# A Hedgehog attention and GLU kernel: the exponentials of the k features as 32 small ScalarE activations per tile, with bias and accumulator

## The chip, the core and the metric

The program runs on one core of a Trainium2 chip. The metric is the device time of one execution in microseconds (us); less is better. The core has five engines, each with its own instruction queue that is worked off in order: TensorE (PE, matmuls), VectorE (DVE), ScalarE (ACT), GpSimd (POOL) and SyncE (SP), which here issues nearly all DMA transfers. An instruction that waits holds up everything behind it on its engine.

## The reference

```python
xn = layernorm(x)                                   # x: 2048 x 1024
q, k, v = split_heads(xn @ wqkv)                    # 32 heads of 32 columns
pq, pk = q @ w_phi, k @ w_phi                       # per head, 32 x 32
phi_q = concat(softmax(pq), softmax(-pq))           # per head: 64 features
phi_k = concat(softmax(pk), softmax(-pk))
kv, z = phi_k^T v, sum_s phi_k                      # per head, over all 2048 rows
s = ((phi_q kv) / (phi_q z + 1e-6)) @ wo
g = silu((sigmoid(xn @ w_gate) * (xn @ w_up)) @ w_down)   # inner width 3584
out = x + s * g
```

The change concerns the two softmaxes of `pk` alone: for each row and head, exp(p - max p) and exp(min p - p) over 32 columns, and the sum of each.

## The kernel before

Everything is fp32. A matrix operand is split into a rounded high part (`L128`, a ScalarE copy) and the rest (`L129`, a VectorE subtraction), and each product takes three matmuls (`mm3`, lines 133 to 135). Each large product is done by seven half-size products (named B11, T2, B21, T3, T1, T4, B22) of sums of blocks; GpSimd makes the sums.

The work runs in stages, with PE's matmuls as the frame: the projections v, k, q of the first half of the rows (chunk 0, from about 20 us), the gate and up products of chunk 0 (28 units of seven ops), the same two stages for chunk 1 (the second gate stage ends at about 1675 us), the down projection with the gate's silu, and attention with the output projection. In the first two kinds of stages PE uses four PSUM banks, in the down projection all eight.

One op of a gate unit is 12 matmuls into one bank. In a unit, B11's sum is copied out of PSUM by ScalarE (`L855`), then B21 accumulates into the same bank, with T2 between them; likewise T4 follows T3 into its bank after VectorE has read it (`L859`), and B22 follows T1 (`L867` or `L874`). Weights stand up to eight ops ahead in a ring of slots.

Small work is spread between the ops as background tasks, by a table of due times (`background`, called behind an op of the gate stage): `k_task` (32 of them, 16 row tiles times 2 halves of 512 columns), `q_features` (32), sums of weights and turns of x. A `k_task` loads a tile of k (`kraw`, one buffer) and of v by DMA, has `features` make the exponentials into `e_k` (one buffer) and the reciprocals of their sums, multiplies, splits features and v into operands and adds the features to `zacc`. The eight matmuls of its products (`L475`) are traced when the next background task begins, and go to the other four PSUM banks. After the last task of a half come `kv_sum`, `kv_blocks` and `z_broadcast`, which use these four banks too.

`features` works on 16 heads of 32 columns, 128 rows: maximum and minimum per head (`L425`, `L426`, VectorE reductions to 128x16), two subtractions of 128x512 with the maximum or minimum broadcast (`L434`, `L435`), one ScalarE exponential of 128x1024 (`L436`), one sum to 128x32 (`L438`) and its reciprocal (`L439`). For k the result lies head by head, first sign and second sign side by side.

A scheduler orders each engine's queue, from the order in which the program is traced and its own estimate of times; so the queues are not in the order of the code. On ScalarE an exponential and a sigmoid need different tables, loaded by an ACT_TABLE_LOAD of 1.28 us.

## Time and profile before

| | before |
|---|---|
| median of 3 runs | 2423.59 us (2423.05 to 2424.21) |
| profiled execution, its own time | 2425.68 us |
| its span, first to last instruction | 2423.9 us |
| granted TensorE clock over the span | 0.993 |
| busy: PE, DVE, ACT, POOL | 97%, 73%, 41%, 41% |
| exponentials of k (`L436`, tile `fc`): 32 | first at 231.8 us, last at 1596.5 us |

A row of a group of instructions gives line, engine, operation, tiles (out <- in, buffer numbers left out), shapes and count, then busy us and the mean ns of one, then the engine's idle time before them and what ended it. A row of a single line gives durations as min/median/max in ns and the first and last start in us. A row of waits gives who waited for whom, the total in us, how often, and the longest. Tile names are those of the slots: `w` weights, `x` the operands of x, `fa`, `fb`, `fc` and `p` the small buffers, `bank` PSUM, `stk` and `stq` the small tiles of k and q features. Durations of neighbours on one engine overlap a little.

### The profile page before, as it was taken

What the parts mean: (1) busy time and instruction counts of PE and PEld (TensorE: products, weight loads), DVE (VectorE), ACT (ScalarE), POOL (GpSimd) and SP (SyncE); (2) the same over time, 40 slices, a digit from 0 to 9 for tenths busy, and PEclk for the clock granted to TensorE, in tenths of its full rate; (3) what the DMA queues carried; (4) which work ended last, traced back from release to release, by engine and by line L of the source; (5) the groups of instructions that cost most, each with busy time, mean ns of one, the idle gap of its engine ahead of it and who ended that gap; (6) DMA issues with size and microseconds to landing.
All of it is one profiled execution on the core that took longest, in us unless ns stands there. A gap on an engine that the chain in (4) does not pass through costs nothing. (4 is left out here: it accounts for less than half of the span.)

```text
span 2423.9 us, 31722 instructions
## 1 busy us (share of the span) xinstructions
PE 2359.0 (97%) x10728; PEld 1952.8 (81%) x10728; DVE 1760.6 (73%) x2341; ACT 996.8 (41%) x1484; POOL 1001.3 (41%) x638
## 2 busy tenths in 40 slices
PE   6999999999999999999999989999999999999998
PEld 4888878788888888887888777878888888788887
DVE  7535797778688764388858998865768786667885
ACT  6432345444454442234534443434333333255442
POOL 4530154757566442002343534343333334322655
PEclk9999999999999999999999999999999999999999
DMA  7874467888888798457898978789668766878664
GB/s 275 268 265 158 160 223 245 287 288 295 302 289 289 260 326 309 154 197 272 301 355 288 310 258 291 263 273 358 212 219 268 244 212 219 279 250 285 215 213 157
DMA packets 262323, 626.17 MB, mean 258 GB/s; under 512 B 37904, under 2 KB 58384, under 8 KB 257552
## 3 DMA queue, kind: packets, MB, share of 16 engines
q1 hardware_dynamic: 262160, 624.15, 75.0%
q8 instruction: 84, 1.38, 0.2%
q14 instruction: 79, 0.65, 0.1%
HBM read 374.47 MB, written 249.56 MB: 257 GB/s over the span
## 5 line engine op out<-in xcount | busy, mean ns | idle before, releaser
L133 PE MATMUL bank<-x,w 128*128 128x512 f32 x2352 | 911.1, 392 | 24.6 <-DVE fc L859 10.0
L134 PE MATMUL bank<-x,w 128*128 128x512 f32 x2352 | 919.4, 391 | 0.0
L135 PE MATMUL bank<-x,w 128*128 128x512 f32 x2352 | 910.1, 391 | 0.0
L129 DVE TENSOR_TENSOR w<-fa,w 128x512 fp32r<-128x512 f32 (+1 forms) x444 | 442.4, 1000 | 215.1 <-ACT w L128 197.1
L133 PEld LDWEIGHTS bank<-x,w 128*128 128x128 f32 x2352 | 443.9, 189 | 124.8 <-DVE fc L859 12.4
L128 ACT CAST w<-fa 128x512 fp32r<-128x512 f32 (+1 forms) x444 | 308.7, 698 | 527.4 <-PE bank L134 348.3
L135 PEld LDWEIGHTS bank<-x,w 128*128 128x128 f32 x2352 | 443.9, 189 | 92.6
L134 PEld LDWEIGHTS bank<-x,w 128*128 128x128 f32 x2352 | 444.3, 189 | 91.5 <-DVE x L129 0.4
L135 PE MATMUL bank<-w,x 128*128 128x512 f32 x708 | 278.1, 393 | 5.8 <-DVE x L129 5.8
L133 PE MATMUL bank<-w,x 128*128 128x512 f32 x708 | 278.5, 394 | 3.2 <-ACT x L128 1.8
L134 PE MATMUL bank<-w,x 128*128 128x512 f32 x708 | 277.4, 392 | 0.0
L613 POOL TENSOR_TENSOR fc<-fc 128x1024 f32<-128x1024 f32 x32 | 82.0, 2563 | 258.4 <-DMA fc<-e_d 116.2
L875 POOL TENSOR_TENSOR fb<-fb,fc 128x512 f32<-128x512 f32 x57 | 90.8, 1592 | 203.1 <-DVE fc L874 203.1
L135 PEld LDWEIGHTS bank<-w,x 128*128 128x128 f32 x708 | 133.7, 189 | 35.4 <-DVE x L129 7.8
L133 PEld LDWEIGHTS bank<-w,x 128*128 128x128 f32 x708 | 133.7, 189 | 32.0 <-ACT x L128 3.0
L134 PEld LDWEIGHTS bank<-w,x 128*128 128x128 f32 x708 | 133.9, 189 | 26.4
L129 DVE TENSOR_TENSOR x<-fa,x 128x512 fp32r<-128x512 f32 x112 | 113.8, 1017 | 36.0 <-ACT x L128 36.0
L334 POOL TENSOR_TENSOR fb<-fa 128x512 f32<-128x512 f32 x28 | 41.8, 1491 | 229.3 <-DMA fa<-w_gu 133.5
L875 POOL TENSOR_TENSOR fc<-fc 128x512 f32<-128x512 f32 x27 | 41.0, 1518 | 230.1 <-ACT w L128 172.4
L129 DVE TENSOR_TENSOR w<-fb,w 128x512 fp32r<-128x512 f32 (+1 forms) x114 | 112.9, 992 | 15.0 <-ACT w L128 14.8
L128 ACT CAST w<-fb 128x512 fp32r<-128x512 f32 (+1 forms) x114 | 70.9, 624 | 120.0 <-PE bank L134 80.9
L128 ACT CAST x<-fa 128x512 fp32r<-128x512 f32 x112 | 69.4, 620 | 75.7 <-DMA fa<-wd_d 38.9
(241 smaller groups left out, 3243.3 us busy)
## 6 DMA issues: line engine op xcount, KB each, us to landing
ws_d<-w SPq DMA_DIRECT2D x112, 512.0 KB, 4.4
w<-ws_d SPq DMA_DIRECT2D x112, 512.0 KB, 5.5
fa<-w_gu SPq DMA_DIRECT2D x84, 512.0 KB, 5.1
fa<-h_d SPq DMA_DIRECT2D x84, 512.0 KB, 4.7
fa<-wf_d SPq DMA_DIRECT2D x32, 1024.0 KB, 5.6
h_d<-fc SPq DMA_DIRECT2D x120, 256.0 KB, 4.6
h_d<-fb SPq DMA_DIRECT2D x76, 256.0 KB, 4.2
fc<-qkv_d SPq DMA_DIRECT2D x64, 256.0 KB, 4.3
```

The costliest lines, as they stand in the source:

```text
L128: nc.scalar.copy(o[0], src)
L129: return nc.vector.tensor_sub(o[1], src, o[0].bitcast(F32))
L133: nc.tensor.matmul(o, a[0], b[0], start=first, stop=False, **kw)
L134: nc.tensor.matmul(o, a[0], b[1], start=False, stop=False, **kw)
L135: nc.tensor.matmul(o, a[1], b[0], start=False, stop=last, **kw)
L334: nc.gpsimd.tensor_add(s1, a21, a22)
L613: nc.gpsimd.tensor_mul(ez, e, zb)
L875: nc.gpsimd.tensor_mul(g, g, b)
```

## The change

For k the two subtractions, the one exponential and the sum are replaced. The maximum is negated (128x16), and then for each of the 16 heads and both signs one ScalarE activation reads 32 columns of the raw k tile, multiplies by 1 or -1, adds the negated maximum or the minimum of its row as bias, takes the exponential and writes the row's sum by the accumulator output. That is 32 activations of 128x32 a task, 1024 in all. For q nothing changes but the place in the code. From line 427 on, line numbers after the change are larger, by 4 from `nc.vector.reciprocal` (`L443`) to the end.

```diff
+        s2, r2 = [st[:, a:a + 2].rearrange("p t h -> p (t h)") for a in (2, 0)]
         if query:
             ev = e.rearrange("p (a t h d) -> p t a h d", a=2, t=2, d=DH)
             pv, mx, mn = [a.rearrange("p (a h) d -> p a h d", a=2) for a in
                           (pv, mx[:, :, None].to_broadcast([P, nh, DH]), mn[:, :, None].to_broadcast([P, nh, DH]))]
+            nc.vector.tensor_tensor(ev[:, 0], pv, mx, op=ALU.subtract)
+            nc.vector.tensor_tensor(ev[:, 1], mn, pv, op=ALU.subtract)
+            nc.scalar.activation(e, e, AF.Exp)
+            nc.vector.tensor_reduce(s2, e.rearrange("p (g d) -> p g d", d=DH), axis=AX.X, op=ALU.add)
         else:
-            ev = e.rearrange("p (h t d) -> p t h d", t=2, d=DH)
-            mx, mn = [a[:, :, None].to_broadcast([P, nh, DH]) for a in (mx, mn)]
-        nc.vector.tensor_tensor(ev[:, 0], pv, mx, op=ALU.subtract)
-        nc.vector.tensor_tensor(ev[:, 1], mn, pv, op=ALU.subtract)
-        nc.scalar.activation(e, e, AF.Exp)
-        s2, r2 = [st[:, a:a + 2].rearrange("p t h -> p (t h)") for a in (2, 0)]
-        nc.vector.tensor_reduce(s2, e.rearrange("p (g d) -> p g d", d=DH), axis=AX.X, op=ALU.add)
+            nc.vector.tensor_scalar(mx, mx, -1.0, None, op0=ALU.mult)
+            ev = e.rearrange("p (g d) -> p g d", d=DH)
+            for h in range(nh):
+                for t, b, scale in ((0, mx, 1.0), (1, mn, -1.0)):
+                    g = 2 * h + t
+                    nc.scalar.activation(ev[:, g], pv[:, h], AF.Exp, bias=b[:, h:h + 1], scale=scale, accum_out=s2[:, g:g + 1])
         nc.vector.reciprocal(r2, s2)
```

The scheduler lays out the queues anew. Three places show it. On ScalarE, in the second gate stage, around the exponential of one k task (`fc` to `fc`; `fb` to `fb` is a q feature's, `p` takes the split of features and of v, `bank_98` holds B11 and then B21), before:

```order
L855 COPY fc_97<-bank_98 128x512
L128 CAST w_93<-fa_95 128x512
L436 ACTIVATE fc_97<-fc_97 128x1024
L128 CAST p_6009<-fc_97 128x8x64
L436 ACTIVATE fb_96<-fb_96 128x1024
L865 ACT_TABLE_LOAD
L865 ACTIVATE fc_97<-bank_98 128x512
```

and of the change, from one B11 copy (`L859` now) to the next:

```order
L859 COPY fc_97<-bank_98 128x512
L128 CAST w_93<-fa_95 128x512
L442 ACTIVATE fc_97,stk_9753<-fc_97,stk_9753 128x32 x32
L128 CAST p_6241<-fc_97 128x8x64
L869 ACT_TABLE_LOAD
L869 ACTIVATE fc_97<-bank_98 128x512
L872 ACTIVATE fb_96<-fb_96 128x512 x2
L128 CAST w_93<-fa_95 128x512 x2
L872 ACTIVATE fc_97<-fc_97 128x512
L434 ACT_TABLE_LOAD
L434 ACTIVATE fb_96<-fb_96 128x1024
L128 CAST p_6241<-fc_97 128x8x128
```

The 32 activations stand as one run behind the B11 copy, in nearly every unit of that stretch, and the unit's sigmoids and most of its casts stand behind them.

On PE, where the last k task's products (`L475`) stand, before, amid the gate stage (`x_0_90,w_93` are B11's operands there, `x_1_642` is one of the next op's):

```order
L135 MATMUL bank_98<-x_0_90,w_93 128x512
L475 MATMUL bank_102<-p_6009 128x256 x2
L475 MATMUL bank_103<-p_6009 128x256 x2
L475 MATMUL bank_104<-p_6009 128x256 x2
L475 MATMUL bank_105<-p_6009 128x256 x2
L133 MATMUL bank_101<-x_1_642,w_93 128x512
```

and of the change, the transposes (`L500`) and the z products (`L520`, `L521`) that follow them, with the last matmul ahead and the first behind (both of the down projection, whose operands take over slots of `x`):

```order
L135 MATMUL bank_105<-x_0_90,w_93 128x512
L500 MATMUL bank_102<-ident,fc_97 128x128 x4
L500 MATMUL bank_103<-ident,fc_97 128x128 x4
L520 MATMUL bank_102<-p_6241,ones 128x512
L521 MATMUL bank_102<-p_6241,ones 128x512
L520 MATMUL bank_103<-p_6241,ones 128x512
L521 MATMUL bank_103<-p_6241,ones 128x512
L133 MATMUL bank_102<-x_0_90,w_93 128x512
```

Before, the last products stand 20.6 ops (of 12 matmuls) ahead of the end of the gate stage, and other matmuls stand between them and each of the later steps. Now they stand 3.7 ops behind it, 28 matmuls of the down projection are between them and the transposes, and none between the steps from the transposes to the z products.

On SP, with what ends each wait, the load of the next raw k tile, before (`L448`; `L372` loads summed weights, `L877` and `L605` store h and q features):

```order
L448 DMA fc_97<-qkv_d 128x512 [waits DMAHW5_49,DVE_49]
L372 DMA w_93<-ws_d 128x1024 [waits PE_49]
L877 DMA h_d<-fc_97 128x512 [waits DMAHW7_49,DVE_49]
L877 DMA h_d<-fb_96 128x512 [waits DMAHW0_49,Pool_49]
L324 DMA fa_95<-w_gu 128x512 [waits DMAHW1_49,DVE_49]
```

and of the change:

```order
L452 DMA fc_97<-qkv_d 128x512 [waits DMAHW1_49,Activation_49]
L609 DMA e_d<-fb_96 128x1024 [waits DMAHW2_49,Activation_49]
L372 DMA w_93<-ws_d 128x1024 [waits DMAHW3_49,PE_49]
L453 DMA fc_97<-qkv_d 128x512 [waits DMAHW4_49,DVE_49]
L572 DMA wd_d<-fb_96 128x512 [waits DMAHW5_49,Pool_49]
```

The load of the next raw k waited for VectorE, which did the last read of the tile in the second subtraction; now it waits for ScalarE, whose last activation of the run reads it.

## The prediction

> **What bounds the kernel now.** The page's first part comes first: which engine is full.
>
> ```profile
> span 2423.9 us, 31722 instructions
> ...
> PE 2359.0 (97%) x10728; PEld 1952.8 (81%) x10728; DVE 1760.6 (73%) x2341; ACT 996.8 (41%) x1484; POOL 1001.3 (41%) x638
> ```
>
> TensorE (PE) is busy for all but 65 us, and the change leaves its matmuls alone. So it can win only where PE waits, and lose only by making PE wait more. Next comes the table by stage, over the three stretches in which the k tasks run (8, 8 and 16 of the 32 tasks have their exponential there), and the longest stretch without any:
>
> ```profile
> 225.00:385.00 160.00, 155.90 (x702) 129.21 (x701) 133.62 (x160) 68.99 (x93) 46.98 (x27) 0.98 0.54 188
> 1040.00:1180.00 140.00, 137.23 (x624) 113.80 (x623) 122.06 (x161) 60.92 (x77) 22.61 (x15) 0.99 0.73 247
> 1270.00:1600.00 330.00, 316.72 (x1426) 260.41 (x1425) 283.98 (x353) 140.59 (x182) 135.75 (x86) 0.99 0.82 281
> ...
> 385.00:1040.00 655.00, 652.00 (x2871) 538.92 (x2870) 453.48 (x590) 276.01 (x380) 330.58 (x223) 1.00 0.79 277
> ```
>
> After the stretch's length the columns are busy time of PE, weight loads, VectorE (DVE), ScalarE (ACT), GpSimd. Where k tasks run, DVE is busy for 84 to 87% and PE idles 4.1, 2.8 and 13.3 us; without them DVE is at 69% and PE idles 3.0 us in 655. ACT has less than half of its time filled everywhere. Who PE waits for, in the first stretch and in the third (line, releaser, us in total, times, longest):
>
> ```profile
> PE bank L133 <- DVE fc L859: 3.7, 1, 3.7
> PE bank L475 <- DVE p L129: 0.4, 1, 0.4
> ```
>
> ```profile
> PE bank L133 <- DVE fc L859: 4.2, 2, 3.1
> PE bank L475 <- DVE p L129: 4.1, 2, 3.3
> PE bank L133 <- DVE fb L867: 3.6, 3, 2.8
> PE bank L133 <- ACT fb L865: 2.3, 2, 1.2
> PE bank L133 <- DVE fc L867: 0.7, 1, 0.7
> ```
>
> So 16.7 us of PE's waits there are ended by DVE: 12.2 by its PSUM evacuations (L859, L867), which stand late in its queue, and 4.5 by the k features' own split.
>
> **What leaves DVE.** Per k task two subtractions and one sum go, and one negation of 128x16 comes. The groups of the third stretch (busy us, mean ns), and the nearest row to the negation:
>
> ```profile
> L438 DVE TENSOR_REDUCE stk<-fc 128x32 f32<-128x1024 f32 x16 | 19.4, 1215 | 14.2 <-ACT fc L436 14.2
> L434 DVE TENSOR_TENSOR fc<-fc,stk 128x512 f32<-128x512 f32 x16 | 16.9, 1056 | 2.6 <-DMA zb_d<-fc 2.6
> ...
> L435 DVE TENSOR_TENSOR fc<-stk,fc 128x512 f32<-128x512 f32 x16 | 14.6, 914 | 0.0
> ```
>
> ```profile
> L168 DVE TENSOR_SCALAR lnw<-mv x13: 140/153/170, 6.2 to 732.0; 128x1 f32<-128x1 f32 x10, 128x2 f32<-128x2 f32 x3
> ```
>
> 19.4 + 16.9 + 14.6 = 50.9 us over 16 tasks is 3.2 us a task; less 0.15 for the negation leaves 3.0. In the third stretch DVE falls from 284 to about 236 of 330 us, 72%, which is about the share of the stretch in which PE hardly waits. Each task therefore takes about 3.0 us out of DVE's queue, and the longest waits for an evacuation are 3.7, 3.1 and 2.8 us: I take off 10.5 of the 12.2. The 4.5 us at L475 I leave, since the features now come later. Bounds: nothing gained (the late evacuations keep standing behind other work) and all 16.7. This term is **-10.5 us**.
>
> **What comes to ACT.** One exponential of 1024 columns becomes 32 of 32 columns, each with a bias per row and an accumulator output; 1024 instructions in all. No such row is in the trace; the nearest:
>
> ```profile
> L436 ACT ACTIVATE fc<-fc 128x1024 f32<-128x1024 f32 x32 | 33.9, 1059 | 56.4 <-DVE fc L435 56.2
> ...
> L178 ACT ACTIVATE fc<-fc,lnw 128x1024 f32<-128x1024 f32 x10 | 12.3, 1243 | 15.7 <-DVE lnw L176 13.3 <-DMA xo_d<-fc 2.4
> ...
> L169 ACT ACTIVATE lnw<-lnw 128x1 f32<-128x1 f32 x10 | 2.0, 203 | 18.0 <-DVE lnw L168 18.0
> ```
>
> ```profile
> 23.33 2.38 ACT L178 ACTIVATE x<-x,lnw 128x1024 f32<-128x1024 f32 x2
> 25.62 0.19 ACT L169 ACTIVATE lnw<-lnw 128x2 f32<-128x2 f32 x1
> 25.70 2.03 ACT L128 CAST x<-bank 128x512 fp32r<-128x512 f32 x4
> ```
>
> An almost empty activation takes 0.20 us; from 1 to 1024 columns it grows by 0.86 us, so 32 columns add 0.03. L178 has two operands per row (scale and bias) and takes 0.18 longer than the exponential: 0.09 for one. Neighbours overlap by about 0.1 (2.38 for two of 1.24). One activation thus occupies ACT for 0.20 + 0.03 + 0.09 - 0.1 = 0.22 us. The accumulator output has no row. From below it is free (0.22); from above it is an instruction of its own of 0.20 that nothing overlaps and that takes the neighbour's overlap away too (0.32 + 0.20 = 0.52). I take it like one more operand per row, 0.10, which is also 0.20 with an overlap: **0.32 us each, 10.2 us a task**, between 7.0 and 16.6.
>
> By the Trainium skill's page "ScalarE: Activation LUTs" (section "What ACT_TABLE_LOAD costs") an activation with a pointer bias takes 280 ns plus 0.833 ns a column and neighbours overlap by 93 ns; for 32 columns that is, as an estimate, 0.21 us and 6.9 us a task, with the accumulator unpriced, so that ACT would not bind at all and the sum would lose its last term. The rows agree with its 93 ns per pointer operand (0.18 for two).
>
> What lies on the path? In the third stretch ACT is busy 140.6 us for 16 tasks, 8.8 each, of which 1.06 is the old exponential; a task has 330/16 = 20.6 us. With the new price ACT has 7.7 + 10.2 = 17.9 of 20.6 us to do: it fits, at 87%. It is full at (20.6 - 7.7)/32 = 0.40 us an activation. What stands behind the burst is the copy of the next unit's B11 sum (L855), the sigmoids and the weights' casts. The copy is the one that PE soon needs: PE runs B11, T2, and then B21 into the copied bank, so it has one op, 12 matmuls:
>
> ```profile
> 1499.77 0.39 PE L134 MATMUL bank<-x,w 128*128 128x512 f32 x1
> ...
> 1500.90 0.39 PE L133 MATMUL bank<-x,w 128*128 128x512 f32 x1
> ```
>
> Five steps in 1.13 us make 0.226 each, 2.7 us an op and 19.0 a unit of seven. The burst starts right behind one copy and ends some 11 us later, with 9 us of other work before the next; up to 2.7 us late it costs PE nothing, and the weights are split up to eight ops ahead, 21 us. I charge **+1.5 us** for the units where a q feature's exponential and two table loads meet the burst.
>
> The first loads of the next k task have to wait too, since the raw k rows are now read until the burst's end:
>
> ```profile
> L448 SPq DMA_DIRECT2D fc<-qkv_d x32: 319/320/451, 167.7 to 1561.7; - x32
> ...
> DMA to landing us min/median/max: 2.6/4.7/7.7
> ```
>
> From task to task that makes 10.2 (burst) + 0.3 (issue) + 4.7 (landing) + 1.2 (two reductions, 0.60 apart in the queue) + 0.2 (negation) = 16.6 us, under 20.6; its cover is 4 us, and beyond that each late microsecond delays the next burst. The load stands in SP's queue, in order: while it waits for the burst, the loads of the summed gate and up weights and the stores of h and of the q features behind it wait too. The weights are fetched up to eight ops ahead, 21 us, which covers that wait of a few us; nothing is charged. Without that cover PE would wait for a weight in each unit.
>
> **What moves at the end of the second gate stage.** The last task's burst now stands behind the last unit's B11 copy, and its products behind down-projection matmuls; before, they stood a good 20 ops earlier. The rows of the work that follows the products:
>
> ```profile
> L475 PE MATMUL bank<-p x256: 277/283/387, 246.0 to 1612.3; 128*128 128x256 f32 x128
> ```
>
> ```profile
> L855 ACT COPY fc<-bank x56: 565/582/590, 307.0 to 1658.6; 128x512 f32<-128x512 f32 x56
> ```
>
> ```profile
> L486 DVE TENSOR_TENSOR fc<-bank,fc x8: 409/413/424, 1188.8 to 1615.0; 128x256 f32<-128x256 f32 x8
> ```
>
> ```profile
> L491 POOL MEMSET fc<- x2: 951/952/954, 1193.9 to 1619.9; 128x1024 f32 x2
> ```
>
> ```profile
> L494 ACT COPY fc<-fc x8: 613/616/621, 1195.0 to 1622.8; 32x512 f32<-32x512 f32 x8
> ```
>
> ```profile
> L519 ACT COPY fc<-bank x4: 589/589/591, 1257.0 to 1665.0; 128x512 f32<-128x512 f32 x4
> ```
>
> Before, the last products (1612.3) had 46 us until the last unit's B11 copy (1658.6), and everything up to L519 (1665.0) hid behind gate matmuls. Now the down projection needs the same four banks. From the products to the last sum (L486) are 3.1 us, memset and four copies add 0.95 + 2.5: 6.6 us, against 28 matmuls in the order between, 6.3 us. From there on PE has nothing else: a copy (0.59), the second half of z split anew (about 0.6 on ACT and 0.7 on DVE), the copy before the banks are free (0.59), and the handovers between engines, about 0.2 each from the gaps in these rows: **+4 us**, between 0 (the queue reached it late anyway) and 12 (memset again late: L494 came 5 us after L486).
>
> **Sum**: -10.5 + 1.5 + 4 = -5 us against the span of 2423.9, which is a run of 2425.7; on the median of 2423.6 that gives 2418.6, and I forecast **2418.5**. DMA bytes do not change. A measurement of this kernel tells 0.2%, 4.8 us, from no change.
>
> **The rivals.**
>
> *ACT is the new bound* (slower). The place is ACT's queue in the third stretch, the mechanism that the burst does not fit a unit, the point 0.40 us an activation. For it: the price of the accumulator is not in the trace, and in-order waits cost room. Against it: the nearest rows make 0.32. At 0.45 a task has 22.1 us of ACT work, 1.5 too much, over 16 tasks 24 us, and at most as much for the other 16, where I take 1 us each; less half the DVE gain, plus the end's 4 us: 2423.6 + 24 + 16 - 5 + 4 = 2463; at 0.42 (21.1 us, 0.5 too much) 2423.6 + 8 + 5 - 5 + 4 = 2436; at 0.52 (24.3 us, 3.7 too much for 32 tasks) 2541.
>
> *The end eats it* (slower). The k chain runs late, since each task's load waits for the burst, and PE stands before the last products. For it: 16.6 of 20.6 us leaves little, landings reach 7.7 us. Against it: the products stand some 11 ops, 30 us, behind their burst, where 15 are needed. At 12 us for the end and 2 us more in the gaps, with a DVE gain of 6: 2431.
>
> *No difference*. The late evacuations were late for other reasons than the k tasks (slow DVE operations beside GpSimd: L434 means 1.06 us and is shortest at 0.68), so that half of the gain goes, and the end takes the rest: -5.5 + 1.5 + 4, 2423.5. That the accumulator sums cost nothing and little else changes ends here as well.
>
> **Chances.** The forecast case 0.45, no difference 0.22, ACT the bound 0.20, the end 0.13. Of the forecast's own range, 2410 to 2422, a sixth lies within 0.2% of before, and a little of the end's. So faster 0.38, same 0.31, slower 0.31. The range reaches down to the whole DVE gain with little at the end, 2409, and up into ACT as the bound at a little under 0.43, 2448; left out are some 0.1 above (a price near 0.52) and less below.
>
> **What the profile after will show.** If the steps hold: 1024 ACT rows of 128x32, some 0.3 us long and 0.32 us apart; ACT busy up by about 290 us to 1290; DVE down by some 80 us; PE's waits for the T3 and T1 evacuations almost gone from the third stretch; waits of about 4 us before the z products at the handover, which weren't there. Wrong, and how: starts 0.40 us or more apart, with PE waiting for the B11 copy behind bursts, mean ACT is the bound; waits of PE for evacuations by DVE that stay at 10 us mean the relief was put in the wrong place; a wait of PE for the k features that grows by tens of us means the chain of single-buffered tasks sets the pace.

## The result and the profile after

| | before | after |
|---|---|---|
| median of 4 runs each | 2423.39 us (2423.05 to 2424.21) | 2452.64 us (2447.78 to 2457.25) |
| ratio after / before | | 1.0122, 95% interval 1.0100 to 1.0144 |
| profiled execution, its span | 2425.68, 2423.9 us | 2455.08, 2453.3 us |
| PE: busy, and the rest of the span | 2359.0, 64.9 us | 2364.8, 88.5 us |

The change made the kernel 1.2% slower; 2418.5 us was predicted, with 2409 to 2448 as the range. Of the 29 us of span, 23.6 are PE standing still and 5.8 are matmuls that took longer. The page's first part, after:

```profile
span 2453.3 us, 33650 instructions
...
PE 2364.8 (96%) x10728; PEld 1952.3 (80%) x10728; DVE 1681.5 (69%) x2277; ACT 1264.8 (52%) x3497; POOL 1003.5 (41%) x638
```

DVE fell by 79 us (some 80 forecast) and ACT rose by 268 (290 forecast). The groups of the new line (busy us, mean ns, then ACT's idle time before it and what ended it), and the first starts of a burst:

```profile
L442 ACT ACTIVATE fc<-fc,stk 128x32 f32<-128x32 f32 x1024 | 312.9, 307 | 58.7 <-DVE p L129 42.6 <-DVE stk L426 8.1 <-DMA w<-ws_d 7.1
L442 ACT ACTIVATION_READ_ACCUMULATOR fc<-fc,stk 128x1 f32 x1024 | 191.9, 187 | 0.0
```

```profile
1407.94 0.32 ACT L442 ACTIVATE fc<-fc,stk 128x32 f32<-128x32 f32 x1 [3.46 <-DVE p L129]
1408.16 0.19 ACT L442 ACTIVATION_READ_ACCUMULATOR fc<-fc,stk 128x1 f32 x1
1408.26 0.31 ACT L442 ACTIVATE fc<-fc,stk 128x32 f32<-128x32 f32 x1
...
1408.56 0.31 ACT L442 ACTIVATE fc<-fc,stk 128x32 f32<-128x32 f32 x1
```

The accumulator output is an instruction of its own, and both overlap their neighbours: 0.305 us from start to start (the median of all that follow one another at once), 9.8 us a burst. The forecast was 0.32 and 10.2. But ACT also stood idle for 58.7 us ahead of bursts, 42.6 of them until VectorE's split (`L129` on `p`) was done. The table by stage, in the stretches of the prediction, after (PE, weight loads, DVE, ACT, POOL, granted clock):

```profile
225.00:385.00 160.00, 154.97 (x703) 127.88 (x702) 105.11 (x133) 119.26 (x513) 46.80 (x28) 1.00 0.53 183
1040.00:1180.00 140.00, 137.81 (x629) 114.35 (x628) 88.38 (x119) 101.41 (x444) 23.12 (x16) 1.00 0.65 220
1270.00:1600.00 330.00, 317.58 (x1415) 261.38 (x1415) 230.28 (x299) 230.53 (x930) 129.00 (x83) 0.99 0.84 285
```

DVE in the third stretch went from 284 to 230 us (236 forecast), and still PE idles 12.4 us there, against 13.3 before. Its waits from 1270 to 1640 us:

```profile
PE bank L479 <- DVE p L129: 7.8, 4, 4.0
PE bank L133 <- ACT fc L859: 3.5, 3, 2.6
PE bank L133 <- ACT fb L869: 1.2, 1, 1.2
PE bank L133 <- DVE fc L861: 1.1, 1, 1.1
...
PE bank L133 <- DVE fb L871: 0.6, 1, 0.6
PE bank L133 <- DVE fc L863: 0.2, 1, 0.2
```

and in the first stretch (225 to 385 us):

```profile
PE bank L133 <- DVE fb L871: 2.1, 1, 2.1
PE bank L479 <- DVE p L129: 2.0, 1, 2.0
PE bank L133 <- DVE fc L863: 0.9, 1, 0.9
```

The late evacuations (`L863` and `L871` now) fell from 12.2 us to 3.8 in these two stretches, much as forecast; waits for the k features (`L479`, the products) came in their place. Over all of 200 to 1760 us little of that is left: PE's waits for VectorE's evacuations of gate sums are 12.3 us there, against 14.5 before. Of them 4.5 are for T2's (`L861`), which had none, and from 385 to 1040 us, where only the last of the first eight k tasks is still at work, they rose from 1.9 to 5.8. The largest single loss is at the end of the second gate stage. PE's waits from 1640 to 1760 us, where it had none at all before:

```profile
PE bank L133 <- DVE fc L490: 7.9, 1, 7.9
PE bank L479 <- DVE p L129: 2.4, 2, 1.2
PE bank L133 <- ACT x L128: 2.0, 2, 1.8
```

And the table by stage there, first before, then after (the last column but two is the granted clock):

```profile
1690.00:1700.00 10.00, 10.00 (x46) 8.28 (x45) 6.51 (x9) 3.19 (x6) 2.78 (x1) 1.00 0.59 211
```

```profile
1690.00:1700.00 10.00, 2.10 (x6) 1.51 (x6) 9.20 (x15) 2.67 (x5) 4.98 (x5) 0.68 0.70 217
1700.00:1710.00 10.00, 8.64 (x32) 6.33 (x30) 1.61 (x4) 4.12 (x8) 5.39 (x6) 0.81 0.45 157
1710.00:1720.00 10.00, 7.77 (x26) 5.77 (x26) 6.72 (x9) 3.77 (x7) 2.40 (x1) 0.83 0.90 314
1720.00:1730.00 10.00, 10.00 (x37) 8.09 (x38) 5.67 (x10) 4.07 (x8) 0.00 (x0) 0.83 1.01 372
```

In these 40 us PE started 101 matmuls; at the 46 in 10 us of before it would have been 184, so some 18 us are lost here. I compared the start of the n-th matmul of the large products in both traces ("lag" from here on: later than before, in us). The lag is 4 from the end of the first gate stage's k tasks on, -12 at 1436 us (VectorE's relief at work), -3 at 1614, 4 at 1672, and 28 at 1726; it ends at 29. So the k stretches brought nothing in the end, and the handover cost 24 us. Some 3 of these are work and not loss: the last eight products, eight transposes and four z products (0.12, 0.11 and 0.23 us from start to start), which stood ahead of this point before.

### The profile page after: what moved, and what is told of

Same layout as the page of the kernel before. It is cut to its first block, busy times and chain, and to the rows that moved or that the text cites. A ratio compares the mean times of both kernels' runs of the same rounds, so it can differ in the third digit from the quotient of the medians.

```text
span 2453.3 us, 33650 instructions
## 1 busy us (share of the span) xinstructions
PE 2364.8 (96%) x10728; PEld 1952.3 (80%) x10728; DVE 1681.5 (69%) x2277; ACT 1264.8 (52%) x3497; POOL 1003.5 (41%) x638
## 5 line engine op out<-in xcount | busy, mean ns | idle before, releaser
L129 DVE TENSOR_TENSOR w<-fa,w 128x512 fp32r<-128x512 f32 (+1 forms) x444 | 440.1, 998 | 200.5 <-ACT w L128 195.6
L442 ACT ACTIVATE fc<-fc,stk 128x32 f32<-128x32 f32 x1024 | 312.9, 307 | 58.7 <-DVE p L129 42.6
L442 ACT ACTIVATION_READ_ACCUMULATOR fc<-fc,stk 128x1 f32 x1024 | 191.9, 187 | 0.0
L129 DVE TENSOR_TENSOR x<-fa,x 128x512 fp32r<-128x512 f32 x112 | 114.2, 1020 | 42.2 <-ACT x L128 41.9
```

The lines of the kernel that those rows point to most:

```text
L129: return nc.vector.tensor_sub(o[1], src, o[0].bitcast(F32))
L442: nc.scalar.activation(ev[:, g], pv[:, h], AF.Exp, bias=b[:, h:h + 1], scale=scale, accum_out=s2[:, g:g + 1])
```

## Experiments

Each ratio is to the kernel before on the same chip, with its 95% interval. The lag of a run is to the trace of before that is used above, with a span of 2423.9 us; on the chips of the runs the kernel before took 2419.0 to 2423.3 us, so a lag is good to some 5 us. The theories, by the names used in the expectations: H, the loss is the handover alone; A, the amount of ScalarE work in these stretches; B, the burst as a block, with the copy of B11's sum (`L859`) behind it; C, the longer way from k task to k task; L, a mere shift of the schedule.

| what was run | median us | ratio (interval) |
|---|---|---|
| 1: change for the first half of the columns only | 2438.27 | 1.0078 (1.0062 to 1.0095) |
| 2: change for the second half only | 2439.63 | 1.0085 (1.0069 to 1.0102) |
| 3: change, k tasks due earlier | 2452.94 | 1.0139 (1.0121 to 1.0156) |
| 4: no shift of k, two exponentials, DVE's sum | 2401.47 | 0.9921 (0.9898 to 0.9943) |
| 5: change, B11 copy on DVE | 2456.13 | 1.0133 (1.0116 to 1.0150) |
| 6: half of the burst | 2411.62 | 0.9950 (0.9935 to 0.9965) |
| 7: no shift, 14.2 us of idle work a task, in small pieces | 2482.66 | 1.0245 (1.0224 to 1.0265) |
| 8: change without the accumulator | 2433.16 | 1.0047 (1.0032 to 1.0062) |
| 9: no shift, idle work in two pieces | 2450.96 | 1.0118 (1.0101 to 1.0135) |
| 10: no shift, idle work in one block | 2461.91 | 1.0164 (1.0147 to 1.0182) |
| 11: as 10, B11 copy on DVE | 2426.46 | 1.0028 (1.0018 to 1.0039) |
| 12: as 3, B11 copy on DVE | 2445.02 | 1.0100 (1.0083 to 1.0117) |
| 13: as 9, B11 copy on DVE | 2419.23 | 0.9987 (0.9974 to 0.9999) |
| 14: as 4, B11 copy on DVE | 2403.04 | 0.9908 (0.9891 to 0.9924) |
| 15: change, k split's subtraction on GpSimd | 2496.33 | 1.0305 (1.0288 to 1.0322) |
| 16: change, both moved | 2436.46 | 1.0070 (1.0051 to 1.0089) |
| 17: no shift for q either | 2403.65 | 0.9926 (0.9906 to 0.9946) |

The kernel before with the due times of its tasks in the second gate stage moved a little took 2424.35 us, 1.0005 (0.9996 to 1.0015), where L would have been 8 us or more away. So this shift of the schedule is worth nothing. It is one other order; what another one can cost is seen in runs 10 and 15.

### Is it the handover? (1, 2, 3)

The tasks of the first half of the columns run in the first two stretches, those of the second half in the third. Runs 1 and 2 make the exponentials of one half in the old way; run 3 pulls the k tasks forward:

```diff
-                    q = max(range(3), key=lambda q: len(rest[q]) / total[q])
+                    q = max(range(3), key=lambda q: len(rest[q]) / total[q] + (0.2 if q == 0 and rest[q] else 0))
```

> The 32 small activations for the first half of the columns only (16 of the 32 k tasks); the second half's tasks as before the change. The last k products then stand 539 ops into the program's PE order, as before the change (563.7 with the whole change). Theory H (handover: the 29 us arise because the last k task ends too late for the down projection, and elsewhere the bursts cost about what VectorE's relief gives): 2421 to 2428 us, no loss at the handover, lag of at most 4 us at any matmul after the first half's tasks. Theory A (ScalarE's queue is too full wherever bursts stand): about half of the loss, 2434 to 2442 us.

> The 32 small activations for the second half of the columns only. The second half starts as early as before the change, and its last products stand at op 546.5, 13.5 ops (37 us) before the gate stage ends. Theory H: 37 us are enough for the work that follows the products (it needs some 15 to 25), so no loss at the handover: 2416 to 2428 us. Theory A: the 16 bursts of the third stretch, one in each unit, are those that crowd ScalarE most, so most of the loss stays: 2438 to 2452 us.

> The whole change, and in the second gate stage the k tasks get earlier due times (a bonus of 0.2 of their share in the list that mixes k tasks, weight sums and q features; weight sums and q features move back). Last products at op 546. Same instructions, same bursts. Theory H: the loss at the handover goes, 2416 to 2430 us. Theory A: bursts as many and denser, 2445 us or more.

In run 3 nothing is lost at the handover (lag 20.7 on both sides of it), and yet the time is the same: its lag was 25 by 1305 us, with one wait of 9.9 us for the copy of B11's sum. Runs 1 and 2 lose nothing there either (14.2 and 15.3 on both sides), and yet each costs about two thirds of what the change costs, together more than the whole; run 1 loses even in the third stretch (lag 4 at 1073 us, 14 at 1614), where its own tasks are of the old kind. Theory H missed in all three and fell as the whole cause: the handover costs only where the k tasks come late, and where they don't, as much is lost elsewhere.

### What the relief of VectorE is worth, and the price of ScalarE's work (4, 6, 7, 8, 17)

Run 4 leaves out the shift by maximum and minimum (exp(k) and exp(-k) over their sums are the same functions, but unprotected against overflow): VectorE is relieved nearly as much as by the change, without the burst. The k task's own way gets shorter too, by the reductions and subtractions ahead of the exponential, so that what run 4 gains is not VectorE's relief alone.

```diff
-        nc.vector.tensor_reduce(mx, pv, axis=AX.X, op=ALU.max)
-        nc.vector.tensor_reduce(mn, pv, axis=AX.X, op=ALU.min)
...
+            for t, scale in ((0, 1.0), (1, -1.0)):
+                nc.scalar.activation(ev[:, t], pv, AF.Exp, scale=scale)
+            nc.vector.tensor_reduce(s2, e.rearrange("p (g d) -> p g d", d=DH), axis=AX.X, op=ALU.add)
```

> The k features' exponentials without maximum and minimum: two activations of 128x512 a task (scale 1 and -1, no bias) that read the raw tile, and the sum on VectorE. A softmax is the same without the shift. VectorE loses two reductions and two subtractions a task (2.4 to 4 us, as much as in the change or more), ScalarE gains 0.2 us instead of 8.7. It shows what VectorE's relief is worth with no burst beside it: if the waits of TensorE for late evacuations go with it, 2403 to 2415 us; if they have another cause, 2419 to 2424 us.

The page of run 4:

```profile
PE 2347.9 (98%) x10728; PEld 1947.6 (81%) x10728; DVE 1689.9 (70%) x2213; ACT 1006.0 (42%) x1518; POOL 992.3 (41%) x638
```

With 8 us more of DVE than after the change, it is 0.8% faster than before (some 19 us), and PE's waits for VectorE's evacuations from 200 to 1760 us are 4.3 us, against 14.5. So the place of the relief was right, and without a burst the relief was worth more than I had put down; against run 4 the change costs 2.0%. Run 6 does one sign in the old way and the other with 16 small activations; it computes all of the reference, and is faster than both kernels, below the ranges of all theories:

```diff
+            nc.vector.tensor_tensor(ev[:, 0], pv, mx[:, :, None].to_broadcast([P, nh, DH]), op=ALU.subtract)
+            nc.scalar.activation(ev[:, 0], ev[:, 0], AF.Exp)
+            nc.vector.tensor_reduce(sv[:, 0], ev[:, 0], axis=AX.X, op=ALU.add)
             for h in range(nh):
-                for t, b, scale in ((0, mx, 1.0), (1, mn, -1.0)):
+                nc.scalar.activation(ev[:, 1, h], pv[:, h], AF.Exp, bias=mn[:, h:h + 1], scale=-1.0, accum_out=sv[:, 1, h:h + 1])
```

> For k the first sign as before the change (subtraction, one exponential, now of 128x512, sum on VectorE), the second sign as 16 small activations with the minimum as bias and the accumulator: bursts of 4.9 us instead of 9.8, half of VectorE's relief. Last products at op 539, as before the change. Theory A and C, in which the cost grows with the burst's length: 2428 to 2438 us. Theory B, in which it counts how far a burst goes beyond the 2.7 us that the copy may be late: 2420 to 2430 us.

Run 7 adds to run 4 (shift left out) 32 idle activations a task with bias and accumulator that nobody reads:

```diff
+        for g in range(32):
+            nc.scalar.activation(idle[:, :DH], ident[:, :DH], AF.Identity, bias=r[:, g:g + 1], scale=1.0, accum_out=idle[:, DH:])
```

> The variant without the shift (2401 us) plus 32 idle activations of 128x32 a task, with a bias per row from the task's reciprocals and accumulator output, whose results nothing reads; they use the identity function, so that they need no table of their own, and the order sets them one by one between the others, off the chain of the k features. ScalarE's amount of work is that of the change. Theory A: 2425 us or more. Theories B and C: no long run in front of the copy and no longer chain, 2396 to 2410 us.

It stands 3.2% above run 4 (1.0245 against 0.9921), with 14.2 us a task in place of the 9.8 of the change, in pieces of 1 to 19 activations. B and C, as they stood then, expected no loss and missed.

Run 8 is the change with VectorE's sum in place of the accumulator:

```diff
-                    nc.scalar.activation(ev[:, g], pv[:, h], AF.Exp, bias=b[:, h:h + 1], scale=scale, accum_out=s2[:, g:g + 1])
+                    nc.scalar.activation(ev[:, g], pv[:, h], AF.Exp, bias=b[:, h:h + 1], scale=scale)
+            nc.vector.tensor_reduce(s2, ev, axis=AX.X, op=ALU.add)
```

> The change without the accumulator output: the 32 activations a task stay, the sum over d is VectorE's again (1.2 us a task, as before the change). Everything of the reference is computed. The pitch should fall from 0.304 to about 0.21 us, 6.9 us a task. Theory A: the line between 4.9 us (2412) and 9.75 us (2453) gives 2429, range 2422 to 2438. Theory B: the block is 6.9 us, the same range. Theory C: the way from task to task is 3 us shorter on ScalarE and 1.2 us longer on VectorE, so 2435 to 2450.

One of its bursts in the timeline:

```profile
1406.46 6.91 ACT L442 ACTIVATE fc<-fc,stk 128x32 f32<-128x32 f32 x32 [0.45 <-DVE p L129]
```

6.91/32 is 0.216 us an activation without the accumulator, where 0.22 was worked out; the accumulator costs 0.09 of the 0.305. With 4.9, 6.9 and 9.8 us of small activations a task (runs 6 and 8, the change) the time is 0.5% under, 0.5% over and 1.2% over before: the loss grows with the burst, though the three differ in VectorE's share too. In run 8 PE waits most for the B11 copy (15.5 us, 5 waits), and little for k features (3.4); C, which expected 2435 to 2450, missed by 2 us. Run 17 takes the shift out of the q features too:

> The q features too without the shift: no maximum, minimum or subtraction in any of the feature tasks; two exponentials with scale 1 and -1 each, and the sum on VectorE. Left out: the shift of all features by maximum and minimum. The q tasks lose about 4 us of VectorE each. If relief of VectorE is what the version without the k shift won (22 us), this wins more: 2385 to 2400; if PE's remaining waits are of other kinds, it stays at 2398 to 2403.

It relieves VectorE by 103 us more and wins nothing over run 4 (0.9926 against 0.9921). Of PE's 13.4 us of waits from 200 to 1760 us in run 4, 8.8 are still ended by VectorE, but less work for it buys no more time.

### By which wait does ScalarE's work cost time? (5, 9, 10, 11, 12, 13, 14)

Run 5 takes the copy of B11's sum out of ScalarE's queue in the change itself:

```diff
-            nc.scalar.copy(u1, bank)
+            nc.vector.tensor_copy(u1, bank)
```

> The whole change, and the copy of each gate unit's B11 sum out of PSUM goes from ScalarE to VectorE (56 copies of 128x512, some 0.67 us each there). Theory B (a burst of 32 activations is one piece of 9.8 us in ScalarE's queue, and what stands behind it, above all the B11 copy that TensorE needs within 2.7 us, comes late): the waits for that copy go (5.4 us in the profile with the change, 13 to 19 us in the last two variants, and the clock that they cost), 2430 to 2442 us. Theory C (the k features come later, since each task's exponentials wait for the task before and last 9.8 us, so TensorE waits for their products and for the work behind the last of them): 2446 to 2458 us. Theory A (the amount of ScalarE's work): 2440 to 2450 us.

It wins nothing, and PE waits for the k features as before (15.7 us), as C expected; this speaks against B by itself in the change. Runs 9 and 10 put idle activations of one column, each with its own place for output and sum, into run 4 (shift left out), so that the work is there without the longer way of the data, as far as the order allows; run 10 traces them with `tc.high_priority()`, which puts them in one block:

```diff
+        for g in range(32):
+            nc.scalar.activation(idle[:, g:g + 1], ident[:, g:g + 1], AF.Identity, bias=ident[:, g:g + 1], scale=1.0, accum_out=s2[:, g:g + 1])
```

> The k features without the shift by maximum or minimum (two exponentials of 512 columns, sum on VectorE, as in the fourth experiment), and behind each task 32 idle ScalarE activations of 1 column with bias and accumulator that nobody reads, each with a place of its own for its output and its sum; the order puts them in two pieces of some 12 and 20 with a cast of the task between them. Left out: the shift; added: the idle work. The pitch should be 0.28 us (0.304 less 31 columns), 8.9 us of ScalarE a task, against 9.75 in the change, without the longer way from task to task. Theory A (the amount of ScalarE work in these stretches): by a line between the half burst (4.9 us, 2412) and the change (9.75 us, 2453) it is 2445, range 2435 to 2455. Theory B (a block that other work cannot pass): two pieces of 3.4 and 5.6 us are no longer than the half burst, 2408 to 2420. Theory C (the longer way from task to task): near the version without the shift, 2401 to 2410.

> The same idle activations, but put in one block of 32, ahead of a cast of the task's own features, so that the way from the task's sums to its products grows by the block, while the loads of the raw rows do not wait for it. Left out: the shift; added: the idle work. Theory A: the same as with the two pieces, within 5 us. Theory B: like the change, 2440 to 2455, clearly above the two pieces. Theory C: the way grows by 8.9 us on one of its two legs, so between, 2410 to 2430, and above the two pieces.

Run 9 costs as much as the change, as theory A said, and run 10 more. In run 9 PE waits 20.8 us for the B11 copy, and also 17.9 for k features: one of the two pieces stands ahead of their cast, so that C is not out of it. PE's longest kind of wait in run 10, and ScalarE's timeline at one of them, with PE's row behind:

```profile
PE bank L133 <- ACT fc L866: 47.4, 9, 10.6
```

```profile
1561.69 0.29 ACT L477 ACTIVATE idle<-ident 128x1 f32<-128x1 f32 x1
...
1570.32 0.28 ACT L477 ACTIVATE idle<-ident 128x1 f32<-128x1 f32 x1
1570.60 1.03 ACT L128 CAST p<-fc 128x1024 fp32r<-128x1024 f32 x1
1571.53 0.57 ACT L866 COPY fc<-bank 128x512 f32<-128x512 f32 x1
```

```profile
1572.16 0.79 PE L133 MATMUL bank<-x,w 128*128 128x512 f32 x1 [10.35 <-ACT fc L866]
```

The whole block stands ahead of the copy (`L866` here), and PE waits for all of it. Runs 11 and 12 move that copy to VectorE, in run 10 and in run 3:

> The version with one idle block of 32 activations a task (2462 us; the shift of the k features is left out, idle work is added), and the copy of B11's sum out of PSUM moved from ScalarE to VectorE. There PE waited 47 us for that copy, in 9 waits. If the copy's place in ScalarE's queue is how the work costs time (theory B), most of the 47 goes, less some 5 us for VectorE's part: 2415 to 2430. If the work is late everywhere and other waits (sigmoids, weights, the k features' products) take its place (theory A): 2445 to 2460.

> The whole change, the k tasks ordered earlier as in the third experiment (2453 us), and the copy of B11's sum out of PSUM moved from ScalarE to VectorE. There PE waited 18.7 us for that copy, in 7 waits, and nothing was lost at the handover. Theory B: 2430 to 2438. Theory A: 2444 to 2456. If the copy matters only with the handover out of the way, 2430 as in B.

Run 11 is 1.4% faster than run 10 (1.0164 to 1.0028, some 33 us): the same ScalarE work costs about half as much once the copy doesn't stand behind it (1.2% over run 14 below, where run 10 stands 2.4% over run 4). That is B, and A as the whole cause fell. Run 12 gained 0.4% on run 3, less than B had expected; its copy waits are gone, but PE waits 12.9 us for k features, and 10.8 us in one piece for an evacuation in the down projection, which B does not explain. Up to that wait run 12 is the best of those with the whole burst: its lag is 5 ahead of the handover and 6 behind it, at 1740 us, where the change has 28. Runs 13 and 14 are run 9 with the copy moved, and the control without idle work:

> The version with the idle activations in two pieces (2451 us; the shift of the k features is left out, 8.9 us of idle ScalarE work a task is added, none of it ahead of the task's own way but for a few us), and the copy of B11's sum out of PSUM on VectorE. If ScalarE's work costs time by the copy behind it (theory B) and, in the change, by the loop of the one feature buffer (theory C), this has neither left: 2403 to 2418. If the amount of work costs by itself (theory A): 2440 or more.

> The control: no shift of the k features (left out as in the fourth experiment), no idle work, and the copy of B11's sum on VectorE. VectorE gets some 10 us more work in the third stretch. All theories: within 6 us of the version without the shift, 2398 to 2407.

Moving the copy costs nothing by itself (run 14 against 4). Run 13 came out 1 us above the range that B and C gave, and 21 us below A's. In run 13 the 8.9 us of work a task are left with a price of 0.8% (against run 14), where with the copy on ScalarE they cost 2.0% (run 9 against 4). So more than half of what idle ScalarE work costs here goes by the copy; but that isn't what the change loses by, since run 5, with 0.9 us more of it a task and the copy moved, stands 1.5% above run 13 (1.0133 against 0.9987, 35 us). They differ in that the burst of the change stands on the k task's own way, with the two reductions and the negation ahead of it. One turn of it, from ScalarE's and VectorE's timelines of the change, in the order of time:

```profile
1407.94 0.32 ACT L442 ACTIVATE fc<-fc,stk 128x32 f32<-128x32 f32 x1 [3.46 <-DVE p L129]
...
1417.62 0.19 ACT L442 ACTIVATION_READ_ACCUMULATOR fc<-fc,stk 128x1 f32 x1
```

```profile
1418.22 1.23 DVE L456 TENSOR_TENSOR fc<-fc,stk 128x1024 f32<-128x1024 f32 x1
```

```profile
1420.73 1.05 ACT L128 CAST p<-fc 128x1024 fp32r<-128x1024 f32 x1
```

```profile
1428.26 2.02 DVE L129 TENSOR_TENSOR p<-fc,p 128x1024 fp32r<-128x1024 f32 x1
```

```profile
1430.31 0.32 ACT L442 ACTIVATE fc<-fc,stk 128x32 f32<-128x32 f32 x1 [6.24 <-DVE p L129]
```

Burst 9.9 us, normalising to 1419.45, cast to 1421.78, and the subtraction, which stands behind other work of VectorE, to 1430.28; the next burst, which writes the same single buffer `e_k`, starts 0.03 us later. 22.4 us for a turn, and ScalarE idle for 6.2 of them. From 1361 to 1669 us fourteen turns take 22.0 us each; before, the same tasks' exponentials came 20.5 us apart. But the subtraction is not the last to be ready in every turn: it ends the wait of 13 of the 32 bursts. In these fourteen turns it was done 21.0 us after the start of its burst, on average, and the next raw tile's minimum (`L426`) 19.2 us after, so the loop of the raw tile is close behind.

### Shortening that turn in the change (15, 16)

Run 15 gives the subtraction to GpSimd, for the k features alone; run 16 moves the copy of B11's sum as well. Both compute all of the reference.

```diff
         nc.scalar.copy(o[0], src)
-        return nc.vector.tensor_sub(o[1], src, o[0].bitcast(F32))
+        return (nc.gpsimd if pool else nc.vector).tensor_sub(o[1], src, o[0].bitcast(F32))
```

> The whole change, with only the subtraction on GpSimd; the copy stays on ScalarE. Everything of the reference is computed. Theory C with B: the last products come some 20 operations earlier and nothing is lost at the handover, but the copies behind the bursts now cost PE as in the versions with idle work: 2432 to 2448, clearly above the run with both. Theory A: 2445 to 2455 in both runs. If the loop alone is the cause: 2415 to 2430 here too.

> The whole change, with the subtraction in the split of the k features (the last but one reader of their buffer) on GpSimd, and the copy of B11's sum out of PSUM on VectorE. Everything of the reference is computed. Theory C with B (the loop of the feature buffer, and the copy behind the burst): bursts come at the 20.6 us that the order gives or sooner, not 22, and nothing is left for PE to wait for but some 16 us of what the idle pieces cost: 2415 to 2430, against 2456 with the copy moved alone. Theory A (amount of ScalarE work): 2440 or more.

With run 5 and the change this makes a square:

| | copy on ScalarE | copy on VectorE |
|---|---|---|
| subtraction on VectorE | 1.0122 (the change) | 1.0133 (run 5) |
| subtraction on GpSimd | 1.0305 (run 15) | 1.0070 (run 16) |

Run 15 was expected at 2432 to 2448 and took 2496. Its first waits, and those of run 16:

```profile
PE bank L133 <- ACT fc L859: 45.1, 9, 11.0
PE bank L133 <- DVE fc L861: 8.1, 4, 2.8
PE bank L479 <- POOL p L129: 6.5, 3, 2.9
```

```profile
PE bank L133 <- DVE fc L878: 6.9, 6, 1.7
PE bank L133 <- DVE fc L859: 6.3, 6, 3.1
PE bank L479 <- POOL p L129: 5.4, 9, 1.8
```

Shortening the turn alone removed the loss at the handover (lag 72.7 on both sides of it) and half of the waits for the features, but the queues came out with bursts ahead of copies, and PE waited 45 us for those. So run 15 is no test of the turn alone; it missed every range that was given for it. With the copy moved too, both waits shrink, the fourteen turns take 20.7 us (21.4 in run 5), and run 16 is 0.5% faster than the change. What the shorter turn takes away there is the handover: the lag of run 5 goes from 16.8 at 1672 us to 29.4 behind it, that of run 16 from 17.1 to 17.6. In the k stretches the two lose the same. So B and C both hold, and either repair alone makes it no better; but together they bring 0.5%, of the 1.2% that the change costs over before and the 2.0% over run 4. Run 16 missed its expectation of 2415 to 2430 by 6 us. What is left there is spread over many short waits, most of them for VectorE.

## Why the prediction was wrong, point by point

**What leaves VectorE: place right, size too small.** -10.5 us for evacuations that came late. These waits fell by 8.4 (12.2 to 3.8), in the third stretch from 8.5 to 0.8, and run 4 shows some 19 us for a like relief without a burst. In the change others of the kind came up outside of these stretches, so that over the program little was gained (14.5 to 12.3).

**The price of an activation: right.** 0.305 us against 0.32, 9.8 us a task against 10.2. By the Trainium skill's page "ScalarE: Activation LUTs" (section "What ACT_TABLE_LOAD costs") an activation of this size, without its accumulator, takes 0.21 us as an estimate from its figures; run 8 agrees with 0.216. The term of the sum that would have gone by that price is ScalarE's +1.5, not the last one, as the prediction has it.

**"It fits, at 87%", +1.5: the step is of the wrong kind.** ScalarE's busy share in the third stretch of the change is 70% (230.5 of 330 us), so it did fit. But fitting says nothing of how long the copy that PE needs is held up by a block of 9.8 us. The 11 and 9 us of the prediction held only for the order that the scheduler happened to choose, in which bursts stand behind the copy: there PE waited 5.4 us for it in the whole program. In the orders of runs 10 and 15 it waited 47 and 45.

**"Task to task 16.6 of 20.6 us, cover 4": the step that failed.** I followed the loop of the raw tile (burst, load, reductions) and left out that of `e_k`, the other single buffer, whose last readers stand behind the burst in two queues: 22.4 us in the turn above, and turns of 22.0 on average, where 20.6 were taken as given. The loop that I did follow was too short as well, 19.2 us up to the minimum where 16.6 had the negation in it, since its reductions stand behind other work of VectorE. And 20.6 is the pace of the third stretch alone: in the second, the first six exponentials came 13.8 us apart before (1045.4 to 1114.3 us), less than my own 16.6, and the six bursts now come 19.8 apart. The products' starts show what follows (second and third stretch, first to last), before:

```profile
L475 PE MATMUL bank<-p x64: 277/283/283, 1060.7 to 1185.6; 128*128 128x256 f32 x64
...
L475 PE MATMUL bank<-p x128: 277/283/387, 1284.2 to 1612.3; 128*128 128x256 f32 x128
```

and after:

```profile
L479 PE MATMUL bank<-p x64: 274/283/388, 1069.7 to 1228.7; 128*128 128x256 f32 x64
...
L479 PE MATMUL bank<-p x128: 277/283/420, 1335.3 to 1689.0; 128*128 128x256 f32 x128
```

From first to last, 125 us became 159 in the second stretch; the third begins 51 us later and ends 77 later. Runs 1 and 2 take this apart: with small activations in the first two stretches alone, the third begins 46 us later than before and ends 14 later; with them in the third alone, it begins 10 later and ends 36 later. So either part alone makes the last products 14 or 36 us late, and both together 77: what comes over from the second stretch is made good only where the third's tasks are of the old kind. The waits for k features, which I left untouched, went from 4.6 to 14.4 us in the whole program, and the last products moved past the end of the gate stage. That they would stand there was read from the order; that the loop has no slack, and that this is why, was not.

**The handover, +4 between 0 and 12: place right, wait and size wrong.** It cost 24 us. At the z products, where 4 us were forecast, PE waited 1.8. The long wait, 7.9 us, stands further ahead, for the banks of the products themselves: from the last product to the last sum (`L490` now) it took 9.4 us where 3.1 were put down. The step took the way from the products to the z products as a chain of its own, but in it ScalarE's second pair of copies (`L489`) stood behind a q feature's exponential, which waited for VectorE's second subtraction (`L433`, of the q feature, done at 1695.34):

```profile
1694.66 0.68 DVE L433 TENSOR_TENSOR fb<-stq,fb 128x512 f32<-128x512 f32 x1
```

```profile
1695.42 1.06 ACT L434 ACTIVATE fb<-fb 128x1024 f32<-128x1024 f32 x1 [5.70 <-issue]
1696.39 0.63 ACT L489 COPY fc<-bank 128x256 f32<-128x256 f32 x2
```

Of the 18 us that were lost from 1690 to 1730 PE stood still for 8.05 in one piece and for 12.2 in all (the gaps between starts of its matmuls); the rest is the granted clock of 0.68 to 0.83. Of the other 6 of the 24, some 3 are the products, transposes and z products that moved behind this point; the other 3 are short waits ahead of 1690 us.

**The rivals.** "ACT is the new bound" set its point at 0.40 us an activation and fell with the price. "The end eats it" named the late k chain and the handover, and was the nearest, with a chance of 0.13; at 2431 it was 22 us too low: it gave the handover 12 us of the 24, and it kept a gain of 6 that was gone by then. The sign that the prediction named for a chain of single-buffered tasks, a wait for the k features that grows by tens of us, showed with 10 us, most of the price being at the handover.

**Open.** That late k tasks cost the 24 us at the handover is shown: in runs 1, 2, 3, 12, 15 and 16 the last products come earlier in the order, or the turn is shorter, and there at most 1 us is lost. That the loops of a task are what makes them late is shown by the turns, and by runs 15 and 16 for `e_k`. How much of the lateness is the loop of `e_k` and how much that of the raw tile is not shown; a second feature buffer, which would test the first by itself, was not run. And the repairs brought only 0.5%: why 8.9 us of ScalarE work a task still cost 0.8% with the copy moved and little of it ahead of the task's own products (run 13 against 14), and why run 16 stands another 0.8% above run 13, was not settled. Only short waits, of several kinds, are left there, so that a part of theory A, the amount of ScalarE's work, stays possible.

## What to carry to other kernels

When one long operation becomes a block of small ones, ask of the new engine not whether its work fits in the time, but what stands behind the block in its queue, with how much slack, and which buffers are held from the block's start until their last reader is through the other queues. Each single buffer makes a loop of its own: sum each one, with the queueing, against the time between tasks where they stand closest, and not against the average of one stretch. And measure a part of such a move as well as the whole: half of the block (run 6) won 0.5%, where the whole lost 1.2%.

## What was not expected of the hardware

The accumulator output of an activation is a second instruction, of 187 ns, which overlaps so far that the pair takes 0.305 us against 0.216 for the activation alone. Where all activations write one and the same place (run 7) the next one starts 0.22 us after the reading of the accumulator began, not 0.10; which of the two places, output or sum, makes the difference was not tried:

```profile
1400.18 0.19 ACT L473 ACTIVATION_READ_ACCUMULATOR idle<-ident,stk 128x1 f32 x1
1400.40 0.32 ACT L473 ACTIVATE idle<-ident,stk 128x32 f32<-128x32 f32 x1
```

A wait of PE can cost more than its length. With 12.2 us of gaps from 1690 to 1730 us the granted clock was 0.68 to 0.83 in all four rows of the table above, and another 6 us went to slower matmuls; before the change the row of 1690 to 1700 us has 1.00. Three times there the matmuls start 0.43 us apart in place of 0.23: for some 5 us behind the gap of 8.05 us, and for some 3 us each from 1711 and 1721 us, behind gaps of at most 2.0. In the whole program PE's busy time grew by 5.8 us with the same matmuls, against 23.6 of standing still. The Trainium skill's page "TensorE: Matmul & The Clock Gate" (section "What's actually happening") says that the clock falls to half after an idle window of about 3.4 us. The fall behind the gap of 8.05 us agrees with that; the two behind gaps of at most 2.0 us came without a gap of that length. The price in these 40 us was half as much again as the gaps themselves.
